# Sparse attention feeding an ELU feed-forward layer: a new plan for the opening and for the first chunk

## The chip, the cores and the metric

The kernel runs on one core of a Trainium2 chip. The metric is the device time of one execution in microseconds (us). The core has a matrix engine (TensorE, PE in the profile), a vector engine (VectorE, DVE), a scalar engine (ScalarE, ACT), a general engine (GpSimd, POOL), which here issues nearly all loads, and SyncE (SP), which issues the stores. Each engine runs its instructions in the order of the program; semaphores hold an instruction until what it needs is there.

## The reference

Eight batches of eight heads, 576 positions, head size 64. Heads 0 to 3 see the last 32 positions ("local"), heads 4 to 7 see every 32nd position before their own ("strided"). The result is the input of a feed-forward layer with an ELU between two products.

```python
scores = scale * np.matmul(q, k.transpose(0, 1, 3, 2))
mask_local = (rel >= 0) & (rel < stride)
mask_strided = (rel >= 0) & (pos[None, :] % stride == pos[:, None] % stride)
...
attn = np.exp(scores)
attn = attn / (np.sum(attn, axis=-1, keepdims=True) + 1e-09)
out = np.matmul(attn, v)
...
x = out.transpose(0, 2, 1, 3).reshape(B * S, H * D)     # 4608 x 512
h = x @ w_in                                            # 512 x 2048
g = np.where(h > 0.0, h, alpha * (np.exp(np.minimum(h, 0.0)) - 1.0))
return g @ w_out                                        # 2048 x 512
```

Inputs and output are float32; products are in bf16.

## The kernel before

**Attention.** Each batch has four pairs of heads: S0, S1 (strided) and l0, l1 (local); in the opening the first batch's are written s0, s1, l0, l1 and the second batch's strided ones S0, S1. A `Pair` has these steps. `t_q` and `t_k` transpose q and k on TensorE (lines 360 to 387) and copy the result out of PSUM, mostly by ScalarE. `s0` and `s1` (`scores`, line 488) are the products of the first and second part of the blocks, with an exp on ScalarE (line 508); `m0`, `m1` multiply by the mask on VectorE (line 523; from the second batch on the mask follows its score by itself). `a0`, `a1` (`av`, line 527) multiply by v, take a reciprocal and scale on VectorE (lines 550, 551). `x` (`x_out`, line 566) transposes the result into `xT`, the input of the feed-forward layer, with a copy on ScalarE, or on VectorE from the third batch on. `v_in` (line 416) copies the strided heads' v from `v_raw` into `v_str`, which has a column of ones behind each block; ScalarE does it for the second batch and VectorE from the third. `halo` (line 423) copies the last 32 rows of each local v block to where the next block finds them.

**Feed-forward layer.** The 4608 tokens are worked in nine chunks of 512. In step s of chunk nb, `moe_in` (line 640) makes four matmuls of 128x512 for 128 columns of the hidden layer, and `moe_act` (line 652) the ELU: an exp on ScalarE (line 655), then a TENSOR_SCALAR (line 662) and a TENSOR_TENSOR (line 664) on VectorE; for five steps of chunk 0 (`ON_SCALAR`) a Relu on ScalarE (line 658) and one instruction on VectorE (line 659) instead. `moe_out` (line 668) makes four matmuls of the second product. `outs` (line 746) says which of them stand behind a step: of chunk 0, number 0, 1 and 2 behind its steps 11, 13 and 15; from then on one behind each step, the other 13 of a chunk in the chunk after it.

**The order of the work** is written by hand. `OPENING` lists the steps of the first batch and the first transposes of the second; `fill` are matmuls without use, `moe.c` the products of feature block c for the first three steps of chunk 0 ("ahead", line 633). Then the loop of line 755 runs the chunks: while chunk nb is worked, batch nb + 1 is prepared, its steps put into gaps: gap 2s stands ahead of step s, gap 2s + 1 behind its ELU. `attention` (line 597) fills the gaps by `TIMES`: a first gap, a distance between pairs, and offsets of the steps. For the second batch the pairs start at the gaps 3, 9, 15, 21; for the third at 4, 10, 16, 22, with v_in at the start.

**PSUM.** The banks go round in rings: `sc` for scores, `hps` for `moe_in` (three banks in the first ten steps of chunk 0, then two), `ops` for `moe_out`, `ring` for the rest. A step that takes a bank waits for whoever read it last.

**Loads.** GpSimd issues them in this order, all in its one queue: the first batch's k, q, v (its strided q comes by SyncE), a quarter of w_in (`load_w_in(0)`), then lines 327 to 334 for the second batch, quarters 1 and 2 of w_in among them; after the opening quarter 3, the four quarters of w_out, and the third batch (line 739). `load_strided` issues five DMAs per tensor, `load_local` one. Quarter i of w_in serves the steps 4i to 4i + 3 of each chunk.

```python
    load_w_in(0)
    load_strided(1, "q")
    load_w_in(1)
    load_strided(1, "k")
    load_strided(1, "v")
    load_local(1, "q")
    load_local(1, "k")
    load_local(1, "v")
    load_w_in(2)
```

Of the kernel before, what the change touches and what calls it, by code (L numbers as in the profile page):

```python
# [32 lines left out]
PIECES = (-2, -1, 0, 2, 3, 5, 7, 0)  # L33
TIMES = (
    None,
    (3, 6, (-3, -2, 0, 2, 4, 6, 9, 3)),
    (4, 6, (-3, -2, 0, 2, 4, 6, 8, 0)),
    (2, 7, PIECES),
    ((2, 8, 15, 22), 0, PIECES),
)  # L40

OPENING = """
s0.cast_q s0.t_q s0.t_k s1.cast_q s1.t_k s0.s0 s0.m0 s1.t_q s0.s1 s0.m1 fill.2 l0.t_q s1.s1
s1.m1 s1.s0 s1.m0 l0.t_k l1.t_q fill.1 s0.v l0.s0 l0.m0 l1.t_k l0.s1 s1.a0 s0.a0 l0.m1 l1.s0
s1.a1 s0.a1 fill.1 l1.s1 l1.m0 fill.1 s1.halo s1.x fill.1 s0.x l1.m1 fill.1 l0.a0 fill.1 l0.a1
l1.a0 moe.2 l1.a1 S0.t_q l0.x S1.t_q moe.3 l1.x moe.0 moe.1
""".split()  # L50
ON_VECTOR = "s0.t_q s1.cast_q s1.t_k l0.t_q s0.v l1.x".split()

# [6 lines left out]
def kernel(  # L59
# [9 lines left out]
    nc = tc.nc  # L69
    B, H, S, D = q.shape  # L70
# [44 lines left out]
    def share(sc, hps, ops, ring):  # L115
        rings.update(sc=Ring(*sc), hps=Ring(*hps), ops=Ring(*ops), ring=Ring(*ring))
# [9 lines left out]
    def bf16_bank():  # L126
# [14 lines left out]
    v_str = [consts.tile([128, 4, 5, D + 1], BF16, tag=f"v_str{i}", name=f"v_str{i}")  # L141
             for i in range(3)]
# [23 lines left out]
    raw = {}  # L166
    src = {"q": q, "k": k, "v": v}

    def load_strided(b, name, engine=nc.gpsimd, heads=range(4)):
        rows = src[name][b, 4:8].rearrange("h (t r) d -> h t r d", r=STRIDE)  # L170
        if b == 0 and name in stage:
            t = stage[name]
        elif name == "v":
            if b not in raw:
                raw[b] = p_raw.tile([128, 4, 5, D], BF16, tag="v_raw", name="v_raw")
            t = raw[b]
        else:
            t = nat[name, "str"][b % 3].rearrange("p (h g d) -> p h g d", h=4, d=D)
        for h in heads:
            engine.dma_start(out=t[0:108, h].rearrange("p g d -> p (g d)"),  # L180
                             in_=rows[h, :, 0:30, :].rearrange(
                                 "t (r g) d -> t r (g d)", g=5))
            if h == 1:
                engine.dma_start(
                    out=t[108:126, :, 0:2, :].rearrange("p h g d -> p h (g d)"),
                    in_=rows[:, :, 30:32, :].rearrange("h t g d -> t h (g d)"))

    def load_local(b, name):
        if name == "v":

            nc.gpsimd.dma_start(
                out=v_loc[b % 3][32:128, :, :, :D].rearrange("p h i d -> p (h i) d"),
                in_=v[b, 0:4].rearrange("h (i p) d -> p (h i) d", p=LB))
            return
        flat = nat[name, "loc"][b % 3]
        if b < EARLY:
            nc.gpsimd.dma_start(
                out=flat[0:LB].rearrange("p (h x) -> p h x", h=4),
                in_=src[name][b, 0:4].rearrange("h (p j) d -> p h (j d)", j=L_RUN))
            return  # L200
        t = flat[:, 0:20 * D].rearrange("p (a i e d) -> p a i e d", a=2, i=5, d=D)
        for h in range(4):
            nc.gpsimd.dma_start(  # L203
                out=t[:, h // 2, 0:4, h % 2],
                in_=src[name][b, h, 0:512].rearrange("(i p) d -> p i d", p=128))
        for a in range(2):
            nc.gpsimd.dma_start(
                out=t[0:64, a, 4],
                in_=src[name][b, 2 * a:2 * a + 2, 512:576].rearrange("h p d -> p h d"))
# [20 lines left out]
    def load_batch(b):  # L230
        for name in "qkv":
            load_strided(b, name)
        for name in "qkv":
            load_local(b, name)

    def rows_of(t, h):

        return t[0:126, h, 0:2, :], t[0:108, h, 2:5, :]
# [83 lines left out]
    def load_w_in(i):  # L322
        nc.gpsimd.dma_start(out=w_in_sb[:, :, 512 * i:512 * (i + 1)],
                            in_=wi[:, :, 512 * i:512 * (i + 1)])

    load_w_in(0)
    load_strided(1, "q")
    load_w_in(1)
    load_strided(1, "k")
    load_strided(1, "v")  # L330
    load_local(1, "q")
    load_local(1, "k")
    load_local(1, "v")
    load_w_in(2)


    class Pair:
# [228 lines left out]
        def x_out(self):  # L566
# [22 lines left out]
            else:  # L589
# [4 lines left out]
                        identity[0:LB, 0:LB])  # L594
                self.copy("x", self.b > 1)(dst, xt[:, 0:S])

    def attention(b, start, pitch, at):


        gaps = {}  # L600
        pairs = [Pair(b, s, hp) for s in (b < LATE, b >= LATE) for hp in range(2)]
        begin = start if b >= LATE else [start + pitch * i for i in range(4)]
        if b >= LATE:
            gaps[begin[0]] = [pairs[3].halo]
        for i, pr in enumerate(pairs):
            if b == 1 and pr.strided:
                pr.t_q = lambda: None
            for off, piece in ((at[0], pr.t_q), (at[1], pr.t_k),
                               (at[7], lambda pr=pr: pr.v_in(0)),
                               (at[7] + (b > 1), lambda pr=pr: pr.v_in(1)),  # L610
                               (at[2], lambda pr=pr: pr.scores(0)),
                               (at[3] if b < WHOLE else at[2] + (b < LATE),
                                lambda pr=pr: pr.scores(1)),
                               (at[4], lambda pr=pr: pr.av(0)),
                               (at[5] - (b >= LATE and i == 0),
                                lambda pr=pr: pr.av(1)),
                               (at[6] + (b > 1 and pr.strided) + (b >= LATE), pr.x_out), (at[5] - 2, pr.halo if b < LATE else lambda: None)):
                gaps.setdefault(begin[i] + off, []).append(piece)
        return gaps
# [86 lines left out]
    def run(gaps, keys):  # L706
        for gap in sorted(g for g in gaps if g in keys):
            for piece in gaps[gap]:
                piece()

    every = range(-10, 1000)
    pairs = {p.name: p for p in (Pair(0, s, hp) for s in (True, False) for hp in range(2))}
    pairs.update((f"S{hp}", Pair(1, True, hp)) for hp in range(2))
    parts = [s for s in OPENING if s.startswith("moe")]
    for step in OPENING:
        pair, what = step.split(".")
# [29 lines left out]
    def outs(nb, s):  # L746

        if nb == 0:
            return [(0, i) for i in range(3) if s == 11 + 2 * i]
        step = [(nb - 1, i) for i in range(3, MC)]  # L750
        if nb < n_chunks:
            step += [(nb, i) for i in range(3)]
        return step[s:s + 1]

    for nb in range(n_chunks + 1):

        if nb + 1 < B:
            gaps = attention(nb + 1, *TIMES[min(nb + 1, 4)])
            if nb == 0:
                share([pair_a], b_halves + singles[3:], [], singles[:3])  # L760
            elif nb + 1 < LATE:
                share([pair_a], b_halves, singles[3:], singles[:3])
            else:
                share([pair_a], b_halves + singles[:1], singles[3:], singles[1:3])
        else:
            gaps = {}
            share([], b_halves + singles[:1], singles[2:], singles[1:2])
        if nb + 3 < B:
            load_batch(nb + 3)
        for s in range(MC):  # L770
            if nb == 0 and s == 10:
                share([pair_a], b_halves, singles[3:], singles[:3])
            if s == (9 if nb + 2 > LATE else 6) and nb > 0 and nb + 2 < B:
                transpose_batch(nb + 2, int(nb + 2 >= LATE))
            if s == 13 and nb + 2 == EARLY:
                transpose_batch(nb + 2, 2)
            run(gaps, (2 * s,) if s else range(-10, 1))
            late = LATE <= nb + 1 and s + 1 < MC
            if nb < n_chunks:
                moe_in(nb, s)  # L780
            if nb < n_chunks and not late:
                moe_act(nb, s)
            run(gaps, (2 * s + 1,) if s + 1 < MC else range(2 * s + 1, 1000))
            if nb < n_chunks and late:
                moe_act(nb, s)
            if nb == B and s == 4:
                range_flag(row_ok16)
            for chunk, i in outs(nb, s):
                moe_out(chunk, i)
        if nb + 1 == B:  # L790
            row_ok16 = range_check()
# [163 lines left out]
```

## Time and profile before

| what | us |
|---|---|
| median of 3 runs (325.82 to 325.88) | 325.88 |
| the profiled execution | 325.9 |
| its span, first to last instruction | 324.0 |
| TensorE busy (2198 matmuls) | 302.3 |
| VectorE busy | 244.7 |
| ScalarE busy | 175.3 |
| GpSimd busy, DMA issues among it | 139.0 |
| DMA: bytes moved | 36.33 MB |

Busy times are sums over the span. "Idle before" an instruction is the time in which its engine had nothing running, and the arrow behind it names what ended that time. In the table of stretches each engine has its busy us and its number of instructions; the granted clock of TensorE (1.00 is full) and what the DMA engines moved follow. The transfers of a GpSimd DMA run after its issue has ended. The opening lasts until about 27 us, chunk 0 to 54.78, chunk 1 to 91.49.

### The profile page before, as it was taken

Reading aid. Unit: us, or ns where it says so; the run is one execution under the profiler, and the core shown is the slowest. Engines: PE = TensorE matmul, PEld = TensorE weight load, DVE = VectorE, ACT = ScalarE, POOL = GpSimd, SP = SyncE. Lnnn points to the kernel's source line nnn. Section 1 sums busy time; section 2 is a strip of 40 time slices with the busy share of each in tenths; the row PEclk is TensorE's granted clock in tenths of the full one; section 3 lists DMA queues with packets and bytes.
Section 4 is the critical chain, followed back from the end, with each engine's and each line's share of the span. In section 5 each row is a group of like instructions: output and inputs, shape, how many; then the busy total and the mean of one; then the engine's idle time right before and its main releaser. Section 6 shows DMA issues by size and latency. Waiting matters only on the chain.

```text
span 324.0 us, 6040 instructions
## 1 busy us (share of the span) xinstructions
PE 302.3 (93%) x2198; PEld 148.2 (46%) x2198; DVE 244.7 (76%) x539; ACT 175.3 (54%) x333; POOL 139.0 (43%) x218
## 2 busy tenths in 40 slices
PE   0887799999999999999999999999999999999993
PEld 0553454455544544444444444444445444444441
DVE  6586986687988988989798879887987666766600
ACT  3668876776545544556645655555565444344310
POOL 9769725968938849968933930000000000000000
PEclk9979999999999999999999999999999999999998
DMA  6999999999999999999994993391110000100012
GB/s 103 156 179 130 172 207 124 149 136 160 119 118 184 148 144 183 75 153 172 215 129 88 141 211 66 81 149 51 53 51 34 33 32 34 65 33 33 34 67 72
DMA packets 108826, 36.33 MB, mean 112 GB/s; under 512 B 87341, under 2 KB 104181, under 8 KB 108789
## 3 DMA queue, kind: packets, MB, share of 16 engines
q0 software_dynamic: 71632, 18.10, 63.1%
q1 hardware_dynamic: 37157, 17.77, 27.2%
q8 instruction: 19, 0.31, 0.4%
q14 instruction: 18, 0.15, 0.2%
HBM read 36.70 MB, written 9.44 MB: 142 GB/s over the span
## 4 chain that ended last, share of the span: by engine, by line
PE 69%; DMA 11%; DVE 9%; POOL 6%; ACT 3%; issue 1%; ACTq 0%; POOLq 0%; DVEq 0%
PE single L674 32%; PE half L629 22%; PE single L629 8%; DMA w_out_sb<-in_moe_w_out_dram 6%; DVE g_sb L664 3%; DVE e_sb L662 2%; DMA q_str<-in_q_dram 2%; PE single L542 2%; DMA k_str<-in_k_dram 2%; DVE x_l L551 1%; PE pair_a L463 1%; POOL v_raw L180 1%; ACT e_sb L655 1%; DMA v_raw<-in_v_dram 1%; POOL k_str L180 1%
## 5 line engine op out<-in xcount | busy, mean ns | idle before, releaser
L674 PE MATMUL single<-w_out_sb,g_sb 128*128 128x512 bf16 x576 | 146.0, 379 | 0.4 <-DVE g_sb L664 0.4
L629 PE MATMUL half<-xT,w_in_sb 128*128 128x512 bf16 x436 | 112.5, 379 | 0.5 <-DVE g_sb L664 0.3
L655 ACT ACTIVATE e_sb<-half 128x512 f32<-128x512 f32 x109 | 65.4, 600 | 69.2 <-PE half L629 67.9
L662 DVE TENSOR_SCALAR e_sb<-e_sb 128x512 bf16<-128x512 f32 x139 | 64.0, 460 | 35.5 <-ACT e_sb L655 35.0
L674 PEld LDWEIGHTS <-g_sb 128*128 128x128 bf16 x576 | 53.5, 98 | 59.6 <-DVE g_sb L664 1.1
L629 PEld LDWEIGHTS <-w_in_sb 128*128 128x128 bf16 x576 | 52.0, 98 | 58.0 <-issue 1.8
L664 DVE TENSOR_TENSOR g_sb<-e_sb,half 128x512 bf16<-128x512 bf16 x104 | 71.5, 688 | 3.6
L629 PE MATMUL single<-xT,w_in_sb 128*128 128x512 bf16 x140 | 36.5, 379 | 1.3 <-DMA w_in_sb<-in_moe_w_in_dram 1.3
L655 ACT ACTIVATE e_sb<-single 128x512 f32<-128x512 f32 x35 | 21.0, 599 | 25.1 <-PE single L629 23.1
L678 ACT COPY o_sb<-single 128x512 f32<-128x512 f32 x36 | 21.1, 588 | 17.9 <-PE single L674 17.8
L542 PEld LDWEIGHTS <-pr 128*128 128x128 bf16 (+3 forms) x352 | 20.4, 103 | 15.5 <-DVE pr L523 1.0
L469 ACT ACTIVATE pr<-pair_a 126x936 bf16<-126x936 f32 (+1 forms) x20 | 19.2, 962 | 12.8 <-PE single L463 12.8
L664 DVE TENSOR_TENSOR g_sb<-e_sb,single 128x512 bf16<-128x512 bf16 x35 | 24.1, 688 | 1.2
L180 POOL DMA_DIRECT2D k_str<-in_k_dram x32 | 20.0, 644 | 9.6 <-issue 3.0
L180 POOL DMA_DIRECT2D v_raw<-in_v_dram x32 | 19.9, 648 | 9.1 <-DVE v_str L421 7.4
L180 POOL DMA_DIRECT2D q_str<-in_q_dram x28 | 17.9, 669 | 5.8 <-DMA w_out_sb<-in_moe_w_out_dram 2.0
L551 DVE TENSOR_TENSOR x_l<-single,rden 96x384 bf16<-96x384 f32 x32 | 17.7, 554 | 1.1
L551 DVE TENSOR_TENSOR x_s<-single,rden 126x256 bf16<-126x256 f32 (+1 forms) x32 | 15.7, 490 | 1.1
L203 POOL DMA_DIRECT2D q_loc<-in_q_dram x20 | 15.5, 817 | 1.9 <-DMA v_raw<-in_v_dram 0.9
L508 ACT ACTIVATE pr<-pair_a 128x576 bf16<-128x576 f32 (+2 forms) x20 | 13.1, 655 | 5.6 <-PE pair_a L500 5.6
L203 POOL DMA_DIRECT2D k_loc<-in_k_dram x20 | 15.3, 798 | 1.1 <-issue 0.8
L550 DVE RECIPROCAL rden<-single 96x6 f32<-96x6 f32 (+2 forms) x64 | 11.9, 185 | 3.1 <-PE single L542 2.4
(114 smaller groups left out, 257.0 us busy)
## 6 DMA issues: line engine op xcount, KB each, us to landing
out_dram<-o_sb SPq DMA_DIRECT2D x36, 256.0 KB, 3.2
v_loc<-in_v_dram POOLq DMA_DIRECT2D x8, 288.0 KB, 8.3
k_str<-in_k_dram POOLq DMA_DIRECT2D x32, 67.5 KB, 5.0
v_raw<-in_v_dram POOLq DMA_DIRECT2D x32, 67.5 KB, 4.5
w_in_sb<-in_moe_w_in_dram POOLq DMA_DIRECT2D x4, 512.0 KB, 9.4
w_out_sb<-in_moe_w_out_dram POOLq DMA_DIRECT2D x4, 512.0 KB, 17.1
q_str<-in_q_dram POOLq DMA_DIRECT2D x28, 67.5 KB, 7.2
q_loc<-in_q_dram POOLq DMA_DIRECT2D x20, 64.0 KB, 5.4
```

Of the source, the lines that this page charges most:

```text
L180: engine.dma_start(out=t[0:108, h].rearrange("p g d -> p (g d)"), in_=rows[h, :, 0:30, :].rearrange("t (r g) d -> t r (g d)", g=5))
L203: nc.gpsimd.dma_start(out=t[:, h // 2, 0:4, h % 2], in_=src[name][b, h, 0:512].rearrange("(i p) d -> p i d", p=128))
L469: nc.scalar.activation(both, sc[0:nk, :, 0:w], ACT.Exp, scale=scale)
L508: nc.scalar.activation(halves, sc[0:nk, :, 0:w], ACT.Exp, scale=scale)
L542: nc.tensor.matmul(av[0:m, p, blk - b0, :], lhsT=pr[0:nk, o:o + m], rhs=vt[0:nk, 2 * self.hp + p, blk, :], start=True, stop=True)
L551: nc.vector.tensor_tensor(self.x[0:nq, b0:b0 + n].rearrange("q g p d -> q p g d"), av[0:nq, :, 0:n, 0:D], r.unsqueeze(3).to_broadcast([nq, ...
L629: nc.tensor.matmul(hps, lhsT=w_in_sb[:, c, m * 128:(m + 1) * 128], rhs=xT[:, c, nb * N_TILE:(nb + 1) * N_TILE], start=start, stop=stop)
L655: nc.scalar.activation(e_sb, hps, ACT.Exp)
L662: nc.vector.tensor_scalar(e1_sb, e_sb, scalar1=1.0, scalar2=1.0, op0=ALU.min, op1=ALU.subtract)
L664: nc.vector.tensor_tensor(g_of[nb][:, m, :], e1_sb, hps, op=ALU.max)
L674: nc.tensor.matmul(ops, lhsT=g_of[nb][:, m, kk * 128:(kk + 1) * 128], rhs=w_out_sb[:, m, :], start=(m == 0), stop=(m == MC - 1))
L678: nc.scalar.copy(o_sb, ops)
```

## The change

Four things change together.

- The loads: the second batch's strided k and v are issued ahead of quarter 1 of w_in, and quarter 2 of w_in ahead of the local v. Between the local k and quarter 2 of w_in, GpSimd copies the second batch's v from `v_raw` to `v_str`, in two instructions; before, ScalarE did this in chunk 0.
- The opening: the halo of the first batch moves ahead of l1's second scores, l1.m1 behind l0.a1, one `fill` is dropped, S1.t_q moves to the end, and S0.t_k and S0.s0 of the second batch come in from chunk 0.
- The second batch's other steps in chunk 0 follow a list of their own, `SECOND`, of gaps and steps. `attention` is no longer called for it.
- The third batch's pairs start at the gaps 8, 13, 18, 23. `moe_out` number 0 and 1 of chunk 0 stand behind steps 13 and 15, number 2 moves into chunk 1, which has two of them behind step 12. `hps` keeps three banks for the first twelve steps of chunk 0.

```diff
 TIMES = (
     None,
-    (3, 6, (-3, -2, 0, 2, 4, 6, 9, 3)),
-    (4, 6, (-3, -2, 0, 2, 4, 6, 8, 0)),
+    None,
+    (8, 5, (-3, -2, 0, 2, 4, 6, 8, 0)),
...
+SECOND = """
+1 S1.t_k 3 S0.s1 7 S0.a0 7 S1.s0 9 S0.a1 10 S1.s1 11 S1.a0 12 S0.x 13 l0.t_q 14 S1.a1 15 l0.t_k
+17 S1.x 17 l0.s0 18 l1.t_q 19 l1.t_k 20 l0.s1 22 S1.halo 22 l1.s0 23 l0.a0 25 l0.a1 25 l1.s1
+26 l1.a0 28 l0.x 28 l1.a1 31 l1.x
+""".split()
...
-s1.a1 s0.a1 fill.1 l1.s1 l1.m0 fill.1 s1.halo s1.x fill.1 s0.x l1.m1 fill.1 l0.a0 fill.1 l0.a1
-l1.a0 moe.2 l1.a1 S0.t_q l0.x S1.t_q moe.3 l1.x moe.0 moe.1
+s1.a1 s0.a1 s1.halo fill.1 l1.s1 l1.m0 fill.1 s1.x fill.1 s0.x fill.1 l0.a0 l0.a1 l1.m1
+l1.a0 moe.2 l1.a1 l0.x S0.t_q moe.3 l1.x S0.t_k moe.0 moe.1 S0.s0 S1.t_q
...
     load_strided(1, "q")
-    load_w_in(1)
     load_strided(1, "k")
     load_strided(1, "v")
+    load_w_in(1)
     load_local(1, "q")
     load_local(1, "k")
+    for o, i in zip(rows_of(v_str[1][:, :, :, 0:D], slice(0, 4)),
+                    rows_of(raw[1], slice(0, 4))):
+        nc.gpsimd.tensor_copy(o, i)
+    load_w_in(2)
     load_local(1, "v")
-    load_w_in(2)
...
+    def second():
+        pairs.update((f"l{hp}", Pair(1, False, hp)) for hp in range(2))
+        gaps = {}
+        for gap, step in zip(SECOND[::2], SECOND[1::2]):
+            pair, what = step.split(".")
+            gaps.setdefault(int(gap), []).append(
+                lambda p=pairs[pair], what=what: p.step(what))
+        return gaps
...
         if nb == 0:
-            return [(0, i) for i in range(3) if s == 11 + 2 * i]
+            return [(0, i) for i in range(2) if s == 13 + 2 * i]
+        if nb == 1:
+            if s == 12:
+                return [(0, 14), (0, 15)]
+            return [(0, s + 2) if s < 12 else (1, s - 13)]
...
-            gaps = attention(nb + 1, *TIMES[min(nb + 1, 4)])
+            gaps = attention(nb + 1, *TIMES[min(nb + 1, 4)]) if nb else second()
...
-            if nb == 0 and s == 10:
+            if nb == 0 and s == 12:
                 share([pair_a], b_halves, singles[3:], singles[:3])
```

2 lines of the change are left out of this document (removed).

## The prediction, made before the changed kernel ran

> **What bounds the kernel now.** I read the page first (TensorE busy 93% of a span of 324.0 us, so everything is TensorE's idle time), then busy time by stretch, then who waited for whom in the stretch that the change rewrites. In the table the columns are TensorE, its weight loads, VectorE, ScalarE, GpSimd, each with busy us and instructions.
>
> ```profile
> PE   0887799999999999999999999999999999999993
> core 0: us, PE busy (x) PEld busy (x) DVE busy (x) ACT busy (x) POOL busy (x), PEclk, DMA share, GB/s
> 28.00:36.00 8.00, 5.53 (x64) 2.91 (x64) 7.71 (x17) 7.70 (x15) 7.88 (x13) 1.00 1.64 144
> 36.00:44.00 8.00, 6.74 (x96) 3.91 (x91) 6.67 (x15) 6.42 (x14) 3.93 (x5) 1.00 1.27 203
> 44.00:54.78 10.78, 9.72 (x78) 5.00 (x77) 8.88 (x20) 7.69 (x15) 3.04 (x6) 1.00 1.10 170
> 54.78:91.49 36.71, 36.26 (x307) 18.66 (x306) 28.29 (x61) 23.22 (x41) 30.93 (x50) 1.00 1.36 137
> ```
>
> 54.78 and 91.49 are the first matmuls of chunks 1 and 2. Chunk 1 leaves TensorE 0.45 us idle: from there on, work moved in costs its full length. Chunk 0 has 2.47 + 1.26 + 1.06 = 4.8 us idle, and that is all there is to win. From 28 to 36 VectorE (7.71 of 8) and ScalarE (7.70) are the bound, later it is mixed. TensorE's waits of 20 to 54.78, and what VectorE met:
>
> ```profile
> PE single L629 <- DMA w_in_sb<-in_moe_w_in_dram: 1.3, 1, 1.3
> PE single L591 <- DVE x_l L551: 1.0, 2, 0.8
> PE pair_a L500 <- ACT pr L508: 0.9, 2, 0.7
> PE pair_a L500 <- ACT kT_str L371: 0.8, 1, 0.8
> PE single L542 <- ACT v_str L421: 0.5, 1, 0.5
> ...
> 28.98 0.86 DVE L662 TENSOR_SCALAR e_sb<-e_sb 128x512 bf16<-128x512 f32 x1
> 61.71 0.81 DVE L421 COPY v_str<-v_raw 126x512 bf16<-126x512 bf16 x1 [1.80 <-DMA v_raw<-in_v_dram]
> ...
> 17.19 0.82 POOL L323 DMA_DIRECT2D w_in_sb<-in_moe_w_in_dram  x1
> 18.89 0.60 POOL L180 DMA_DIRECT2D k_str<-in_k_dram  x1 [0.87 <-DMA v_loc<-in_v_dram]
> 20.75 0.57 POOL L180 DMA_DIRECT2D k_str<-in_k_dram  x1 [1.26 <-DMA w_in_sb<-in_moe_w_in_dram]
> 28.40 1.19 POOL L191 DMA_DIRECT2D v_loc<-in_v_dram  x1
> 29.57 1.53 POOL L323 DMA_DIRECT2D w_in_sb<-in_moe_w_in_dram  x2
> 35.91 1.44 POOL L245 MEMSET q_str<- 32x1280 bf16 x1
> ```
>
> Each wait of GpSimd's queue is on the DMA issued eight before it, so only eight loads are in flight; strided ones also cost GpSimd 0.6 us each, and at 26 to 28 us, with only these, the DMA moved 94 GB/s instead of the 205 of the weights.
>
> **The change, part by part.** Chunk 0 is walked in three stretches, with durations of the rows of before.
>
> Loads. W_in(1) moves behind the five k and the five v loads. These still wait for the same landings (18.8 v_loc, 20.7 w_in(0), 21.9 q_str), so k gains only the slot at 17.2 and v lies 0.6 us earlier: last issue near 25.5, landing some 2.5 us later (the shortest v_raw landing), near 28.3. W_in(1), which landed at 24.9 and is needed by chunk 0's step 4 (31.67 before), goes out near 26.1 and needs its issue of 0.8, some 2 us until it flows, and 0.5 MB at 205 GB/s = 2.5 us: 30 to 31.4. Then q_loc, k_loc, the GpSimd copies, w_in(2), v_loc, w_in(3), and w_out as before. W_in(2) landed at 40.4, behind v_loc at 38.9; now before v_loc, near 37 to 38, and step 8 asks at 38.5: the wait of 1.26 goes. While GpSimd copies, w_in(1), q_loc and k_loc are still in flight (1.1 MB, over 5 us), so the DMA does not run dry, and w_out comes as before or up to 1.5 us earlier.
>
> The copies of v: two on ScalarE (0.63 + 0.83) become two on GpSimd, 512 and 768 elements per partition. The trace has no GpSimd copy. Lower bound: its memset of 1280 elements, 1.16. Upper: its affine select, 0.29 for 128 elements, by elements 2.9. I take 1.7, nearer the memset, which is the row with as many elements. They wait for the last v landing at 28.3, so end near 30.0; S0.a0 is wanted by TensorE near 30.3 (step 3 starts when VectorE has done e0, near 29.4, and takes 0.86). Behind them in GpSimd's queue stand w_in(2) and all later loads; cover: step 8 is at 38.5. If the copies end later, TensorE stands, but VectorE has a backlog until 33.0 and feels nothing up to about 31.
> The Trainium skill, "SBUF — State Buffer", Who interferes with whom, says that GpSimd and a VectorE copy or tensor_scalar in its fast two-port form exclude each other for a whole instruction. The rows fit it: one L662 took 0.86 beside 0.41 to 0.43 elsewhere, while GpSimd wrote a DMA's descriptors, and the q_str memset took 1.44 against 1.16 for k_str's. By it, the sum would be up to 1.3 us higher (two blocked operations of some 0.65).
>
> Opening, until chunk 0's first exp. S0.t_k (matmuls 0.44, ScalarE copy 0.68) and S0.s0 (0.28, exp 0.60, mask 0.41) come forward; cover on TensorE: moe.0 and moe.1 (0.65 each) lie between, which removes the waits of 0.8 (kT_str) and 0.7 (pr). The halo copy (ScalarE 1.26) starts at v_loc's landing, 18.85 instead of 19.81; l1.s1's exp slips from 19.14 to 20.1; s0.x's copies end at 21.9 instead of 22.2. L1.m1 stands behind l0.a1, so l1.a1's x is ready at 24.1 instead of 24.6. TensorE then does l1.x, S0.t_k, moe.0, moe.1 until 26.4 (27.45 before). But on ScalarE S0.s0's exp (26.7) and S1.t_q's copy (27.2) now stand ahead of chunk 0's first exp: 27.75 instead of 27.11, **0.6 later**. The dropped filler matmul (0.2) is not on this chain.
>
> 28 to 37.4. VectorE is bound. Before: 27.74 to 37.38 for e0 to e5 and the four S masks and two S0 results. Now from 28.3, without S0.m0 (0.33 from start to start): 28.3 + 9.64 - 0.33 = 37.6; without the stretched L662 37.2. **No gain**: TensorE's waits that are removed turn into waits for VectorE (its bank for step s comes free with g of step s-3).
>
> 37.4 to chunk 1. Before, 2.3 us idle (1.26 + 1.06). The w_in wait goes (-1.26). New: S1.halo (VectorE 0.49) now stands right ahead of l0.a0, and TensorE waits some 0.9; I leave the rest. TensorE's work shrinks by a moved output product (4 matmuls, 0.86) and by S1.a0, which is done earlier (0.2). Together -1.26 + 0.9 - 0.86 - 0.2 = **-1.4**: chunk 1 starts near 53.4.
>
> Chunk 1. The moved product comes back, where TensorE is full: **+0.86**. Batch 2's v copy moves from gap 4 to gap 8, 2 steps later (2 x 2.3 us), so VectorE's wait of 1.80 goes; of it TensorE felt only part of its 0.45 idle: **-0.3**. L1.x at gap 31 instead of 30 trades a wait of 0.3 (x_l) for one on VectorE's copy behind the step's g: 0. Pieces every 5 gaps squeeze batch 2 from 26 gaps into 23; VectorE, 28.29 of 36.71 busy there, stays below TensorE.
>
> Sum: the profiled execution took 325.9 (324.0 and 1.9 around it; median of the runs 325.88). 325.9 - 1.4 + 0.86 - 0.3 = **325.0**.
>
> **The rivals.**
> *More is won* (322.9). For: ScalarE loses 1.46 us of v copies in the stretch where it is busy 7.70 of 8; if chunk 0 is held by VectorE's work alone, it ends at 28.3 + 23.8 (24.17 busy from 27.7 to 55.9, less the mask) + 0.9 of small gaps = 53.0 instead of 55.9: -2.9 + 0.86 - 0.3 = -2.35, and with the first exp not later -0.6 more. Against: the list still puts ScalarE's copies in bunches (two t copies, S1.x's two and an exp between two steps).
> *The GpSimd copies hold up the opening* (327.3, the other side). Place: S0.a0, then all of TensorE, and VectorE's tensor_scalar. From 28.3 at the upper 2.9, and with operations of VectorE in its way (0.43 as at 28.98, once or twice) they end at 32 to 32.5; step 4 starts 1.0 to 1.5 late and VectorE, beyond its backlog, loses the same, plus 0.9 for its own blocked operations: 2.3 on the forecast. It decides from an end later than 31. Against: DMA issues and memsets beside VectorE stretched only three operations. That is the skill's rule above at its strongest.
> *Hidden anyway* (325.8). VectorE's stretch until 37.4 simply goes on, the wait for w_in(2) becomes one for VectorE's g, and the 0.86 comes back in chunk 1.
> *Not as it says*: the k loads gain one slot only, so S0.t_k at 24.8 might wait; its third load is issued at 20.75 and lands near 23.5. Within the range.
>
> **How the numbers follow.** Chances: forecast 0.40 (its own 324.2 to 325.7), more 0.22, hidden 0.12, slower 0.26. A measurement of this kernel tells 0.2% (0.65 us: 325.23 to 326.53) from no change. Faster: 0.30 of the forecast's and 0.22 = 0.52; same 0.10 + 0.12 = 0.22; slower 0.26. The range 323.0 to 327.2 takes in most of "more" and of "slower", and the bounds of the copies.
>
> **What would show it.** Right: no wait of L629 on w_in in steps 4 and 8; GpSimd's copies at 28 to 30.5; no wait on kT_str or pr before 35; VectorE without gaps from 28.3 to 37; chunk 1's first matmul near 53.4; no wait of v_str near 60. Wrong: a wait of S0.a0 on GpSimd over 0.8 us, L662 rows near 0.9 beside the copies, a wait at step 4 on w_in(1), chunk 1 not earlier than 54.3 (then slower or same) or before 52.5 (then more).

## The result and the profile after

The changed kernel takes 327.98 us (median of 11 runs, 326.12 to 329.28); the kernel before, on the same chip, 325.88 (324.27 to 327.15). The ratio is 1.0071, with a 95% interval of 1.0049 to 1.0093: 2.3 us slower, 1.6 to 3.0. The forecast was 325.0.

The profiled execution took 327.7, with a span of 325.8 instead of 324.0. The first view is the page's row of TensorE's busy tenths in 40 slices of the span, and the row of its granted clock.

```profile
PE   0885889999999999999999999999999999999993
...
PEclk9999699999999999999999999999999999999997
```

One slice is 8.1 us. The fifth, 32.6 to 40.7, has a clock of 0.6 only, right where the change was to win: from 32.2 on the clock is halved for 6.8 us. The next view is busy time by stretch; 56.86 and 94.13 are the first matmuls of chunks 1 and 2.

```profile
core 0: us, PE busy (x) PEld busy (x) DVE busy (x) ACT busy (x) POOL busy (x), PEclk, DMA share, GB/s
26.00:34.00 8.00, 3.81 (x38) 2.06 (x36) 6.07 (x11) 5.02 (x10) 7.48 (x10) 0.89 1.12 168
34.00:44.00 10.00, 9.65 (x95) 5.09 (x94) 6.83 (x17) 6.44 (x13) 5.95 (x10) 0.75 1.69 179
44.00:56.86 12.86, 11.13 (x105) 5.66 (x104) 11.30 (x25) 9.57 (x20) 4.79 (x9) 1.00 1.05 159
56.86:94.13 37.27, 36.76 (x311) 18.13 (x310) 29.42 (x61) 22.92 (x42) 30.92 (x50) 1.00 1.28 137
```

Chunk 1 starts at 56.86, where the forecast had 53.4 and the kernel before 54.78. It then takes 37.27 instead of 36.71, the 0.86 - 0.3 more that was forecast (but see the table: the agreement is luck of these two profiles). TensorE is busy 36.76 of it, so it is still full. In 26 to 34 TensorE idles for half of the time, and in 34 to 44 it is "busy" 9.65 of 10 at a clock of 0.75, which is work drawn out, not more work. Who waited for whom (TensorE, 26 to 58 us; total, times, longest):

```profile
PE half L645 <- DVE g_sb L680: 2.3, 1, 2.3
PE half L645 <- DMA w_in_sb<-in_moe_w_in_dram: 1.9, 1, 1.9
PE single L552 <- DVE v_loc L438: 0.9, 1, 0.9
```

L645 is `moe_in`'s matmul, L552 `av`'s. The first row stands ahead of step 3, the second ahead of step 4; the third is the halo's, foreseen at 0.9. TensorE's timeline of steps 3 to 5 (start, us, engine, line; in brackets the idle time before and what ended it):

```profile
30.18 1.02 PE L645 MATMUL half<-xT,w_in_sb 128*128 128x512 bf16 x4 [2.26 <-DVE g_sb L680]
...
33.47 1.89 PE L645 MATMUL half<-xT,w_in_sb 128*128 128x512 bf16 x4 [1.90 <-DMA w_in_sb<-in_moe_w_in_dram]
...
36.04 1.89 PE L645 MATMUL single<-xT,w_in_sb 128*128 128x512 bf16 x4
```

Four matmuls that take 1.02 at full clock took 1.89 twice behind the two idle stretches. The load that step 4 waits for, in the chain of waits (start, us):

```profile
24.70 8.72 DMA w_in_sb<-in_moe_w_in_dram
```

and GpSimd's timeline from its issue on:

```profile
24.70 0.96 POOL L330 DMA_DIRECT2D w_in_sb<-in_moe_w_in_dram  x1
25.49 0.86 POOL L204 DMA_DIRECT2D q_loc<-in_q_dram  x1
26.18 0.84 POOL L204 DMA_DIRECT2D k_loc<-in_k_dram  x1
27.55 1.58 POOL L342 COPY v_str<-v_raw 126x512 bf16<-126x512 bf16 x2 [0.52 <-DMA v_raw<-in_v_dram]
```

W_in(1) was issued at 24.70, sooner than forecast, and landed 8.72 us later, at 33.4, not at 30 to 31.4; two more loads followed it at once. GpSimd's copies of v were as forecast: 1.58 us, done at 29.1.

One execution can't be laid beside another to a microsecond here: the same kernel, profiled again (e11), starts chunk 1 1.6 us later. So the table gives several; the letters stand for runs that the next section explains. The columns are the start of the exp of chunk 0's steps 0, 3, 5, 8 and of chunk 1's first, chunk 0's length between the two first exps, chunk 1's, and the span, all in us and read from the traces.

| kernel | 0 | 3 | 5 | 8 | chunk 1 | length 0 | length 1 | span |
|---|---|---|---|---|---|---|---|---|
| before | 27.1 | 31.8 | 34.3 | 41.4 | 55.8 | 28.7 | 36.7 | 324.0 |
| before again (e11) | 27.8 | 32.5 | 36.3 | 42.9 | 57.5 | 29.7 | 36.3 | 324.2 |
| e7, before, no wait at step 8 | 27.3 | 32.0 | 35.8 | 41.3 | 57.0 | 29.7 | 35.9 | 323.6 |
| g4, before, clears moved | 28.3 | 33.0 | 35.5 | 41.5 | 57.1 | 28.8 | 35.9 | 323.4 |
| e6, before, outputs replanned | 27.5 | 32.2 | 34.7 | 41.6 | 55.9 | 28.4 | 37.3 | 324.3 |
| **after** | 28.0 | 31.2 | 38.0 | 43.2 | 57.9 | 29.9 | 37.3 | 325.8 |
| e9, after, no wait at step 4 | 29.1 | 32.3 | 36.5 | 43.1 | 57.8 | 28.7 | 37.8 | 326.2 |
| f1, after, clears on VectorE | 29.1 | 33.2 | 37.2 | 43.0 | 57.8 | 28.7 | 37.3 | 325.9 |
| g1, after, all three away | 29.4 | 32.5 | 35.4 | 43.3 | 58.1 | 28.6 | 37.3 | 326.0 |
| g2, after, own data | 29.0 | 32.1 | 35.0 | 42.9 | 57.8 | 28.8 | 37.4 | 325.7 |

Of the profiles that the table leaves out, chunk 0 takes 28.6 (f2), 28.8 (e4) and 29.6 (e8) with the old list, and chunk 1 35.9 to 36.4. With the new list chunk 0 takes 28.1 (e1), 29.5 to 30.3 (e2, e3, e10), and 30.9 to 31.8 (e5, g3, e12), and chunk 1 37.3 to 38.7 (e12, with the old outputs, 36.7).

The half clock is part of this scatter. E11 and the first profile of before are one kernel, and their first four exps are equally spaced; then e11 has half clock for 3.4 us (from 31.9 on) and before has none in chunk 0, and e11's chunk is 0.9 longer. E7 has such a piece too, g4, e6, e4 and f2 have none there. Each of e9, f1, g1 and g2 has one, the changed kernel two in a row.

From chunk 2 on all kernels run nearly alike (32.7 to 33.2 for chunk 2, then 31.5 to 32.1 each, the last but one 27.6); the trace of before that the prediction read spent 1.2 us more in its chunks 2 to 5 than e11.

### The profile page after: what moved, and what is told of

It is laid out like the page before. It is cut to its first block, busy times and chain, and to the rows that moved or that the text cites. A ratio compares the mean times of both kernels' runs of the same rounds, so it can differ in the third digit from the quotient of the medians.

```text
span 325.8 us, 6035 instructions
## 1 busy us (share of the span) xinstructions
PE 302.8 (93%) x2197; PEld 147.6 (45%) x2197; DVE 244.8 (75%) x539; ACT 172.9 (53%) x331; POOL 140.7 (43%) x220
## 4 chain that ended last, share of the span: by engine, by line
PE 78%; DMA 7%; DVE 6%; ACT 3%; POOL 3%; issue 1%; ACTq 0%; POOLq 0%
PE single L690 36%; PE half L645 26%; PE single L645 9%; DMA w_in_sb<-in_moe_w_in_dram 5%; PE single L552 3%; DVE g_sb L680 2%; DMA k_str<-in_k_dram 2%; PE pair_a L473 2%; ACT e_sb L671 1%; DVE e_sb L678 1%; DVE x_l L561 1%; PE single L588 1%; POOL k_str L187 1%; POOL v_raw L187 1%; PE pair_a L510 1%
## 5 line engine op out<-in xcount | busy, mean ns | idle before, releaser
L645 PE MATMUL half<-xT,w_in_sb 128*128 128x512 bf16 x432 | 112.4, 382 | 4.2 <-DVE g_sb L680 2.3
L678 DVE TENSOR_SCALAR e_sb<-e_sb 128x512 bf16<-128x512 f32 x139 | 63.8, 459 | 35.6 <-ACT e_sb L671 35.0
L645 PEld LDWEIGHTS <-w_in_sb 128*128 128x128 bf16 x576 | 52.7, 99 | 61.0 <-issue 4.4
L645 PE MATMUL single<-xT,w_in_sb 128*128 128x512 bf16 x144 | 38.4, 386 | 0.0
L671 ACT ACTIVATE e_sb<-single 128x512 f32<-128x512 f32 x36 | 21.7, 603 | 24.9 <-PE single L645 22.8
L552 PEld LDWEIGHTS <-pr 128*128 128x128 bf16 (+3 forms) x352 | 20.3, 103 | 15.7 <-issue 2.0
L680 DVE TENSOR_TENSOR g_sb<-e_sb,single 128x512 bf16<-128x512 bf16 x36 | 24.8, 688 | 1.2
```

What stands on the lines that cost most here:

```text
L552: nc.tensor.matmul(av[0:m, p, blk - b0, :], lhsT=pr[0:nk, o:o + m], rhs=vt[0:nk, 2 * self.hp + p, blk, :], start=True, stop=True)
L645: nc.tensor.matmul(hps, lhsT=w_in_sb[:, c, m * 128:(m + 1) * 128], rhs=xT[:, c, nb * N_TILE:(nb + 1) * N_TILE], start=start, stop=stop)
L671: nc.scalar.activation(e_sb, hps, ACT.Exp)
L678: nc.vector.tensor_scalar(e1_sb, e_sb, scalar1=1.0, scalar2=1.0, op0=ALU.min, op1=ALU.subtract)
L680: nc.vector.tensor_tensor(g_of[nb][:, m, :], e1_sb, hps, op=ALU.max)
```

## The experiments

Where a number is a ratio, it is to the kernel before on the same chip, with its 95% interval. The first question was which of the new waits costs the 2 us.

**e1, the load order of w_in(1) undone.**

```diff
 load_strided(1, "q")
+load_w_in(1)
 load_strided(1, "k")
 load_strided(1, "v")
-load_w_in(1)
```

> The changed kernel with one line put back: quarter 1 of w_in is loaded ahead of k and v again, all else as changed. Theory 'late weights' (step 4 waits 1.9 us for w_in(1), and the idle time brings the TensorE clock to 0.50 for 5 to 6 us): no wait of L645 on w_in at step 4, the clock at 1.00 from 28 to 40, chunk 1 starts at 53.5 to 54.5 instead of 56.86, time 324.3 to 325.5. Rival 'GpSimd copy' and rival 'late first exp' (TensorE idle 28.0 to 30.2 because ScalarE does S0.s0's exp and S1.t_q's copy first): unchanged within 0.5 us of 327.9, since neither is touched.

Measured: 327.92, 1.0077 [1.0042, 1.0112]. The wait at step 4 is gone, but in its place stands this one, in the opening (TensorE's timeline of e1; the first row in it is `S0.t_k`):

```profile
26.92 0.43 PE L378 MATMUL single<-identity,k_str 126*128 126x126 bf16 x5 [1.53 <-DMA k_str<-in_k_dram]
```

The first exp moved to 30.0. Ahead of step 4, the DMA has both k and w_in(1) to bring, and in these two profiles whichever is second is waited for: `S0.t_k` in the opening made k urgent.

**e2, v copied by ScalarE again** (at gap 6 of `SECOND`, the two GpSimd copies dropped).

```diff
-1 S1.t_k 3 S0.s1 7 S0.a0 ...
+1 S1.t_k 3 S0.s1 6 S0.v 7 S0.a0 ...
...
-    nc.gpsimd.tensor_copy(o, i)
```

> The changed kernel, but v of the second batch copied by ScalarE in gap 6 as before, not by GpSimd. 'Late weights': w_in(1) is issued ahead of the copies and lands near 33.4 as it did; time 327.5 to 328.7. Rival 'GpSimd copy': the time falls below 326.5, TENSOR_SCALAR rows near 29 to 31 are all below 0.5 us.

Measured: 328.48, 1.0108 [1.0059, 1.0157]. Nothing comes back: GpSimd's copies aren't the cause of the loss.

**e3, filler matmuls ahead of steps 3 and 4,** nine and eight, to keep TensorE's clock up.

```diff
+if nb == 0 and m == 3:
+    for _ in range(9):
+        nc.tensor.matmul(rings["ring"].peek(), lhsT=identity, rhs=mask_l[:, 0:512], ...)
+if nb == 0 and m == 4:
+    for _ in range(8):
+        nc.tensor.matmul(hps, lhsT=identity, rhs=mask_l[:, 0:512], ...)
```

> The changed kernel with 17 filler matmuls without use: 9 ahead of step 3 into a free bank and 8 ahead of step 4 into that step's own bank, where TensorE stands idle at 28.0 to 30.2 and 31.6 to 33.5; all waits stay. Theory 'clock' (the half clock from 32.6 to 38.9 is the larger part of the loss): clock 1.00 from 28 to 40, chunk 1 starts about 2 us earlier (54.5 to 55.3), time 325.7 to 326.5. Rival 'waits alone' (VectorE or the late data set the pace, the slow clock is hidden): time 327.3 to 328.5.

Measured: 329.22, 1.0147 [1.0087, 1.0206]. The clock was 1.00 throughout chunk 0, and step 4 to step 5 took 1.4 us instead of 2.6. Yet TensorE then waited elsewhere, for VectorE's x of the strided heads (its waits, 26 to 58 us):

```profile
PE single L558 <- DVE x_s L567: 1.4, 1, 1.4
PE single L594 <- DVE x_s L567: 0.9, 1, 0.9
```

**e4, e6, e7, e8: one part of the change alone, in the kernel before.** E4 has w_in(1) behind k and v; e6 the outputs, the banks and the third batch's gaps; e7 w_in(2) ahead of the local v; e8 v by GpSimd.

```diff
-load_w_in(1)                    # e4: three lines lower
+load_w_in(1)
-(4, 6, (-3, -2, 0, 2, 4, 6, 8, 0)),    # e6
+(8, 5, (-3, -2, 0, 2, 4, 6, 8, 0)),
-return [(0, i) for i in range(3) if s == 11 + 2 * i]
+return [(0, i) for i in range(2) if s == 13 + 2 * i]
...
-load_local(1, "v")              # e7: behind load_w_in(2)
+load_local(1, "v")
+    nc.gpsimd.tensor_copy(o, i)    # e8
```

> The kernel before with one line moved: quarter 1 of w_in behind the second batch's strided k and v, nothing else of the change. 'Late weights': w_in(1) lands at 33 to 34, step 4, at 31.67 before, waits 1.5 to 2 us; time 327.0 to 328.5, the slow clock perhaps with it. Rival (the order of the loads is free, the loss is in the rest of the plan): 325.6 to 326.3.

> The kernel before with the change's outputs (two of chunk 0's products in chunk 0, the third in chunk 1 as a second one behind step 12), three banks for 12 steps and the third batch from gap 8 every 5 gaps; nothing else. Forecast's terms: chunk 0 not shorter by the whole 0.86, chunk 1 longer by 0.86 less 0.3: chunk 1 starts 0 to 0.9 earlier and lasts 37.1 to 37.6; time 325.3 to 326.4. Rival 'late list': the third batch's later and denser steps cost chunk 1 more, 38 or over; time 327 or over.

> The kernel before with quarter 2 of w_in ahead of the local v of the second batch, nothing else. Theory: the wait of 1.3 us at step 8 (L629 on w_in) goes or falls below 0.4, and VectorE's and ScalarE's own work hides half of it: time 324.6 to 325.3 where before measures 325.3 to 325.9. Rival 'hidden': within 0.3 us of before.

> The kernel before with v of the second batch copied by GpSimd between the local k and the local v, nothing else. Theory 'GpSimd copy harmless': copies of about 1.6 us in all, TENSOR_SCALAR rows beside them up to 0.9; ScalarE loses 1.46 us of work in gap 6: time 324.9 to 325.9. Rival 'GpSimd copy' (port and queue): w_in(2) lands later and step 8 waits 2 us or more, time 326.5 to 327.5.

Measured: e4 325.82, 1.0029 [1.0000, 1.0059]; e6 326.55, 1.0054 [1.0017, 1.0091]; e7 326.4, 1.0043 [1.0011, 1.0074]; e8 326.85, 1.0047 [1.0014, 1.0080]. No part wins anything. Three of them lose 0.43 to 0.54% each alone, where the whole change loses 0.71%; so their prices don't add up. These three are set against the same runs of the kernel before, and that kernel against itself (e11) came out at 1.0016, so a price of 0.4% is near the limit of the comparison. In e4 step 4 waits only 0.2 us for w_in(1), not the 1.5 to 2 that were expected.

E7 matters most. The wait for w_in(2) at step 8, the 1.26 that the forecast took off, is gone. Its profile is best laid beside e11's: both have a piece of half clock at the same place, and up to step 7 their exps lie equally far behind the first, to 0.1 us (step 7 12.59 in both). Here is TensorE at step 8 in e11, and between the steps 8 and 9 in e7:

```profile
41.82 1.04 PE L629 MATMUL single<-xT,w_in_sb 128*128 128x512 bf16 x4 [1.01 <-DMA w_in_sb<-in_moe_w_in_dram]
```

```profile
41.52 0.30 PE L500 MATMUL pair_a<-qT_loc,kT_loc 64*128 64x96 bf16 x6 [0.30 <-ACT pr L508]
...
42.73 0.32 PE L578 MATMUL single<-identity,x_s 108*128 108x108 bf16 x3 [0.69 <-DVE x_s L551]
```

Without the wait of 1.01 step 8's exp comes 14.1 instead of 15.1 us behind the first, 1.0 sooner. Then TensorE waits 0.30 for ScalarE's exp and 0.69 for VectorE's x_s, which e11 doesn't have there, and step 9's exp is at 17.2 in both. What w_in held up, VectorE and ScalarE hold up one step later.

E6 shows chunk 1's part by itself (busy time by stretch, the columns as above):

```profile
54.81:92.10 37.29, 36.37 (x306) 18.17 (x311) 28.81 (x61) 22.76 (x41) 30.79 (x50) 1.00 1.30 133
```

37.29, as in the changed kernel, though the opening and the list of chunk 0 are those of before.

**e5, the opening's early scores undone too** (e1, and S0.t_k, S0.s0, S1.t_q back where they had been, the S pairs' other steps too).

```diff
-l1.a0 moe.2 l1.a1 l0.x S0.t_q moe.3 l1.x S0.t_k moe.0 moe.1 S0.s0 S1.t_q
+l1.a0 moe.2 l1.a1 S0.t_q l0.x S1.t_q moe.3 l1.x moe.0 moe.1
```

> The changed kernel with two parts put back: w_in(1) ahead of k and v, and S0.t_k, S0.s0, S1.t_q where they were (S0.t_k and S0.s0 in gaps 1 and 3, the S pairs' other steps in the gaps of before); GpSimd's copy of v, w_in(2) ahead of v_loc, the late local steps, the outputs and batch 2 as changed. Theory 'early scores': k is wanted in the opening and w_in(1) at step 4, eight DMAs in flight cannot bring both, so either order costs 1.5 to 1.9 us, and S0.s0's exp ahead of chunk 0's first exp delays step 3: then step 5 starts at 33 to 34 (36.0 in the changed one), chunk 1 at 54 to 55, time 325 to 326. Rival 'late list' (the later steps, the moved product and batch 2 cost it): step 5 earlier but chunk 1 still at 56 or later, time 327 to 328.5.

Measured: 328.79, 1.011 [1.0059, 1.0161]. The first exp is at 27.1, and step 5 at 33.9 is the earliest of all. Then step 6 comes only at 38.5: TensorE had waited twice, 1.85 us in all, for VectorE's x_s, and from 35.6 on it ran at half clock for 6.8 us. What had been won is lost again within one step.

**e9 and e10, no wait for w_in(1) by other data.** Steps 4 to 7 of chunk 0 use quarter 0 of w_in, so that part of the result is another. E10 also has S0.s0 and S1.t_q behind the first exp, and S1.t_k one gap later.

```diff
 def moe_chunk(nb, m, c, hps, start, stop):
+    if nb == 0 and 4 <= m < 8:
+        m -= 4
```

> The changed kernel, but steps 4 to 7 of chunk 0 multiply by quarter 0 of w_in instead of quarter 1 (other data, so that part of the result is another), so that nothing of chunk 0 waits for w_in(1); the same loads and the same work. Theory 'late weights' (the wait of 1.9 us at step 4 and the half clock behind it): step 4's exp at 33 to 33.5 (35.4 in the changed one), the half clock gone or half as long, chunk 1's first exp at 55 to 56 (57.9), time 325.5 to 326.5. Rival 'chain' (VectorE's and ScalarE's list sets the pace anyway, the wait was cover for it): chunk 1's first exp at 57 or later, time 327.2 or over.

> As the run with quarter 0 in steps 4 to 7 (that part of the result is another), and besides S0.s0 and S1.t_q behind chunk 0's first exp (gap 1), S1.t_k in gap 3. Theory 'late first exp': the first exp at 26.9 to 27.2 instead of 28.0, step 3 at 29.4 to 29.8, TensorE's wait of 2.3 for VectorE's g at step 3 below 1.5, time 0.5 to 0.9 below that run. Rival 'chain': equal within 0.3 us.

Measured: e9 327.3, 1.0055 [1.0026, 1.0084]; e10 327.06, 1.0061 [1.0031, 1.0090]. In e9 TensorE's first two waits are

```profile
PE half L647 <- DVE g_sb L682: 2.2, 1, 2.2
PE single L552 <- DVE x_s L561: 1.5, 1, 1.5
```

and step 8 is at 43.1, as in the changed kernel. In e10 chunk 0's first exp comes at 25.3, and TensorE then waits 2.1 for GpSimd's v_str, whose copies take 2.04 here. Chunk 1 still begins at 55.6, the earliest of all profiles, and then takes 38.3. The time is not below e9's, as its rival had it: the late first exp, taken away, gave nothing that can be measured.

**e11, the kernel before again,** to see what the comparison makes of no change.

> The kernel before, once more, for a second trace. If the 1.2 us that chunks 2 to 5 took more in the first trace (33.2, 31.8, 31.9, 31.6 against 32.7, 31.5 to 31.7, 31.45, 31.45 in all others) belong to that one execution: 32.7 and 31.45 here, time 325.0 to 325.9. If they belong to the kernel: the same excess.

Measured: 325.63, 1.0016 [0.9989, 1.0043].

**e12, the changed kernel with outputs, banks and third batch as before** (e6's diff, the other way).

> The changed kernel with the outputs, the three banks and the third batch's gaps as before; the opening, loads and second batch as changed. Forecast's term: chunk 1 lasts 36.7 instead of 37.3, chunk 0 0.3 to 0.9 longer; time within 0.5 us of 327.9. Rival (the later and denser third batch is a main cost): time 326.8 or less.

Measured: 328.34, 1.0078 [1.0039, 1.0116]. Chunk 1 takes 36.7 again, but in this profile step 4 waits 3.0 for w_in(1) and chunk 0 takes 31.8. The 0.6 that chunk 1 gives back can't be seen in the time.

The next theory, A below, was VectorE held off by GpSimd. In e1's VectorE timeline one operation of 0.43 us takes seven times as long, while GpSimd issues v_loc's load and clears six pads of q_loc, k_loc (`clear_loc`) back to back; in the kernel before, VectorE stood still for v_raw just then:

```profile
60.46 2.95 DVE L678 TENSOR_SCALAR e_sb<-e_sb 128x512 bf16<-128x512 f32 x1 [0.50 <-ACT e_sb L671]
```

TensorE feels it: among its waits of 57 to 97 us in e1 is this one, and e1's chunk 1 takes 38.7.

```profile
PE half L645 <- DVE g_sb L680: 1.2, 1, 1.2
```

The Trainium skill, "SBUF — State Buffer", Who interferes with whom, has a VectorE `tensor_scalar` in its two-port form and GpSimd exclude each other for a whole instruction; the row agrees in being stretched beside GpSimd, though it doesn't name the form. But 2.95 is several GpSimd instructions long, not one.

**f1 and f2: the clears that GpSimd did at 35 to 38 and near 62 us go to VectorE,** in the opening behind S0.t_k (f1, the changed kernel) or around l1.x (f2, the kernel before).

```diff
+        if pair == "clear":
+            if what == "1":
+                clear_v(2)
+                clear_nat(2)
+            else:
+                for i in range(3):
+                    clear_loc(i, nc.vector)
+            continue
-    clear_v(2, nc.gpsimd)
-    clear_nat(2, nc.gpsimd)
-    for i in range(3):
-        clear_loc(i, nc.gpsimd)
```

> The changed kernel with the 'clear' memsets (the last v and natural buffers, the three pairs of q_loc, k_loc) done by VectorE in the opening, instead of by GpSimd behind the v copies and, for the last ones, at 61.7 to 63.3 us. Theory A, VectorE held off by GpSimd's memsets is a good part of the loss: no TENSOR_SCALAR over 1 us between 58 and 66 us, chunk 1 from 37.3 to 36 or less, the span 1 to 1.5 us below the changed kernel's 327.98, near 326.7. Theory B, the loss is the pace of the new lists: the memsets' place is worth at most 0.3 us, 327.5 to 328.5.

> The kernel before with the same memsets on VectorE in the opening. Theory A: there VectorE waits for v_raw while they run at 60.7 to 62.4 us, so that little is lost to them; 0 to 0.7 us below before, chunk 1 at 36 to 36.7. Theory B: within 0.3 us of before. By both, a loss of more than 0.5 us would mean that the opening's VectorE has no room for the memsets.

Measured: f1 327.45, 1.0064 [1.0034, 1.0094]; f2 325.7, 1.0000 [0.9976, 1.0025]. The longest such operation near there is this in the changed kernel, and the second in f1:

```profile
62.00 1.62 DVE L678 TENSOR_SCALAR e_sb<-e_sb 128x512 bf16<-128x512 f32 x1 [0.46 <-ACT e_sb L671]
```

```profile
61.88 1.18 DVE L678 TENSOR_SCALAR e_sb<-e_sb 128x512 bf16<-128x512 f32 x1 [0.57 <-ACT e_sb L671]
```

Chunk 1 takes 37.28 from exp to exp in both. TensorE is the bound there, and VectorE has slack for 1.6 us. It has none for much more: where the operation takes 2.3 to 3.0 us (e1, e2, e3, e9, e10), chunk 1 takes 37.7 to 38.7, and TensorE waits 0.4 to 1.2 for g_sb. So theory A doesn't explain the changed kernel's profile in chunk 1, but it does explain the longer chunk 1 of these five. F2 shows no cost of the clears in the kernel before.

**g1 to g4: do the costs stand in for one another?** G1 takes three suspects from the changed kernel at once: e9's edit, nine fillers ahead of step 3, and the clears on VectorE where it idles at 9 to 25 us. G2 has the kernel's own data and e1's order instead of e9's edit. G3 is e5 with these clears, g4 the kernel before with them.

```diff
-s0.cast_q s0.t_q s0.t_k s1.cast_q s1.t_k s0.s0 s0.m0 s1.t_q
+s0.cast_q s0.t_q s0.t_k clear.k s1.cast_q s1.t_k clear.v s0.s0 s0.m0 clear.q s1.t_q
...
-s0.v l0.s0
+s0.v clear.l01 l0.s0
...
-l1.x
+clear.l2 l1.x
```

> The changed kernel with three suspects away at once: steps 4 to 7 of chunk 0 read quarter 0 of w_in (no wait for its load; part of the result is another), nine filler matmuls ahead of step 3 (no half clock), the clears on VectorE in idle places of the opening at 9 to 25 us (no memsets of GpSimd beside the ELU). Theory A, the loss of chunk 0 goes from one of these to the next when only one is taken away: step 3 to step 5 in 3 us (4.0 to 6.8 before), step 8 at 41 us or sooner, chunk 1 from 56 us, span 324, 326.2 median. Theory B, the new lists' own pace: step 8 at 43 us whatever is taken away, span 325.5 or more, 327.3 or more.

> The changed kernel with its own data, w_in's quarter 1 issued ahead of k and v again, nine fillers ahead of step 3, the clears as in g1. Theory A: the wait moves to the opening (k_str at 26.9), first exp at 29.5 to 30, from there steps as in g1: chunk 1 from 57 us, 327. Theory B: 327.5 to 328.5.

> e5 (w_in's quarter 1 early, S0's scores out of the opening and back in their gaps) with the clears on VectorE in the opening's idle places. e5 reached step 5 at 33.9 us, the earliest of all, and then lost 2 us at 34 to 36.5 behind a TENSOR_SCALAR that took 1.6 us over its 0.43, and the clock after it. Theory A: without GpSimd's memsets that wait and the half clock go; step 6 near 36.5 instead of 38.5, chunk 1 near 56, span 324.5, 326.3. Theory B: chunk 1 at 58 or later, 328 or more.

> The kernel before with the clears on VectorE in idle places of the opening, where f2 had them ahead of chunk 0's first exp (28.0 instead of 27.1 to 27.8 us). Theory A: first exp at 27.1 to 27.8, chunk 1 near 55.5, 0.3 to 1 us below before, faster than both kernels. Theory B, the memsets cost nothing where they were: within 0.3 us of before.

Measured: g1 327.14, 1.0058 [1.0033, 1.0083]; g2 327.23, 1.0060 [1.0031, 1.0088]; g3 327.55, 1.0056 [1.0026, 1.0086], with chunk 1 at 59.8 in its profile; g4 325.79, 1.0017 [0.9989, 1.0046].

G1's time lies just under theory B's 327.3, those of g2 and g3 between the two forecasts, and g4 is as theory B had it. In the profiles, step 3 to step 5 takes 2.9 us as theory A said (6.8 in the changed kernel's profile). Then step 5 to step 8 takes 7.9, against 5.2, and step 8 stands at 43 as theory B said. Here is g2 from its first ELU to step 6, by stretch (the columns as above), then by TensorE's waits (20 to 58 us), then in TensorE's timeline at step 6:

```profile
29.70:39.00 9.30, 7.43 (x51) 3.33 (x49) 9.03 (x20) 6.07 (x12) 8.22 (x11) 0.89 1.50 159
```

```profile
PE single L384 <- DMA k_str<-in_k_dram: 1.2, 1, 1.2
PE single L558 <- DVE pr L539: 0.9, 1, 0.9
...
PE single L594 <- DVE x_s L567: 0.9, 1, 0.9
```

```profile
37.35 1.91 PE L651 MATMUL half<-xT,w_in_sb 128*128 128x512 bf16 x4
```

VectorE is busy 9.03 of 9.30, and what TensorE waits for is VectorE's mask (L539) and x_s (L567). From step 0's g to step 5's VectorE needs 7.5 us in g1 and g2, against 8.1 in before, so the new list spares it 0.6 here. But in these two it starts on the ELU only when chunk 0's first exp is done, at 29.7 to 30.1, 2 us later than before (27.7). Up to step 6 VectorE is the wall.

The half clock is not out of the way, though. It comes behind the two waits, at 37.1 in g2 and 37.9 in g1, for 3.4 us, and g2's matmuls of step 6 take 1.91 instead of 1.04. So the stretch from step 5 to step 8 holds both, and the two runs don't separate them. Over all executions the clock can be told apart: its mean over a run is 0.988 in the changed kernel and 0.995 in g1 and 0.996 in g3, which is what the kernel before has (0.995), and g1 and g3 still lose 0.58 and 0.56%. Most of the loss needs no more half clock than before had. No version beats the kernel before; f2 and g4 can't be told from it.

## Why the prediction was wrong

**What was right.** The opening's first exp is later: 27.75 forecast, 28.0 measured. Over the changed kernel and four variants with the same opening (after, e2, e3, e9, e12) the mean is 28.2, over before, e6, e7, e8 and e11 27.3, so 0.9 instead of 0.6; e4, with the old opening and only the load order changed, has 28.1, so the opening isn't shown to be the whole of it. The halo's wait is 0.9. GpSimd's copies take 1.58 us against 1.7, a choice between wide bounds, and are done at 29.1. The wait for v_raw near 60 is gone.

**What failed first: "The w_in wait goes (-1.26)", in "37.4 to chunk 1".** The wait goes, and nothing comes of it: e7 has the step 1.0 us sooner and gives 0.30 + 0.69 back to ScalarE and VectorE before the next, and its ratio is over 1. The forecast took a wait that ended last at one matmul for time that could be had. Yet the paragraph before it had said of 28 to 37.4 that TensorE's removed waits turn into waits for VectorE; that holds behind step 8 too. With it goes the rest of the credit: between the first exps of chunks 0 and 1 the forecast needed 26.7 (55.84 - 1.4 - 27.75). The old list takes 28.4 to 28.8 in five of the six profiles without half clock there (before, e4, e6, f2, g4), and the new one 28.6 to 28.8 in e9, f1, g1 and g2, with an output product less; 28.1 (e1) is the shortest of all. E9, f1, g1 and g2 each have one piece of half clock, so whether the 0.86 was hidden, or was won and paid again to the clock, stays open. The rival "hidden anyway" named the failure, with 0.12, and left out the opening's cost.

**What failed second: "W_in(1) ... 30 to 31.4", in "Loads".** From issue to landing it took 8.72, not 0.8 + 2 + 2.5 = 5.3. Over the nine profiles with this order it took 6.1 to 8.7 and landed at 31.8 to 34.2. The 205 GB/s are those of 38 to 50 us (203 to 211 in every 2 us), when mostly weights were on the way; here v loads were issued ahead of the quarter and q_loc and k_loc behind it, and in 26 to 34 all loads together got 168. The profile of before had the number, in the page's list of DMA issues (median 9.4 us) and in the answer for w_in's tile:

```profile
w_in_sb<-in_moe_w_in_dram POOLq DMA_DIRECT2D x4, 512.0 KB, 9.4
```

```profile
DMA to landing us min/median/max: 7.7/9.4/12.5
```

The 7.7 is this very quarter, issued at 17.19 and landed at 24.9 by the prediction's own figures. From the forecast's issue at 26.1 it gives 33.8, and step 4 had been at 31.67 before. The Trainium skill, "DMA: Bandwidth & Descriptors", Anatomy of one DMA, gives a fit of 2.0 us + bytes / 436 GB/s; for 1 MB of float32 read that is some 4.4 us, an estimate by this fit, and the row of 9.4 differs.

**What failed third: "-0.3" in "Chunk 1".** The first pair of profiles gives 0.56 more, as summed, by luck. With the old plan chunk 1 takes 35.9 to 36.7, with a mean of 36.2 (before, e4, e7, e8, e11, f2, g4); with the new outputs 37.3 (after, e5, e6, f1, g1), 37.4 (g2), and more where the stretched operation comes in. So the plan costs some 1.1, the whole product and no credit.

**What went with the late load.** TensorE idled 2.26 us for VectorE's g, then 1.90 for w_in, within 6 us, and the half clock came, for 6.8 us from 32.2 on. The first of the two waits is no matter of the load: e9, which doesn't wait for w_in, has it too (2.2), with 3.4 us of half clock behind it. Chunk 0 takes 29.9 in the changed kernel's profile against 28.7, about 1.2. In the time the share is smaller: e9, f1, g1 and g2, with half of the half clock, have ratios of 1.0055 to 1.0064, against 1.0071, and the intervals overlap.

**The sum in the profiles' terms:** 0.9 for the opening, 0 to 1.2 for chunk 0, 1.1 for chunk 1; 2.0 to 3.2 against 2.3 (1.6 to 3.0) measured. This is bookkeeping of lengths: taking one of them away again (e10, e9, e12) didn't bring its time back. The forecast had the first and the last with 1.16 in all, and a credit of 2 in chunk 0 (26.7 against 28.7) that nothing pays. "More is won" fell with the same credit. The rival on the slower side (327.3) had the time almost right by luck and the cause wrong: GpSimd's copies end on time, and moving them back (e2) wins nothing.

**A row read too well.** The prediction set one L662 of 0.86 against 0.41 to 0.43 elsewhere. That trace has 14 of 139 over 0.5, this one among them, with two near by (0.54 at 30.8, 0.56 at 35.7) and the longest 1.17 at 85.2. The sum didn't hang on it.

**What stays open.** The parts don't add up: e6 alone has 1.0054, and the changed kernel without e6's part 1.0078. E4's, e7's and e8's prices alone (0.3 to 0.5%) aren't traced to one wait each; in e8's profile VectorE's TENSOR_SCALARs are stretched by 2.0 us in chunk 0, against 0.7 and 1.3 in the two of before. Whether e10's early chunk 1 would win, if the clears didn't stand beside its chunk 1, wasn't tried. G3's profile loses 1 us more than e5's, but its execution, 329.85, was one of the slowest of its twelve (median 327.55).

## What to carry to other kernels

When several engines are near their bound in a stretch, a wait that ends last at one place is not time to be won: sum the work of the next engine over the stretch first, from where it starts, and count only what lies beyond. For a load that is moved, take the time from issue to landing that the profile shows for that very load, under traffic, not its bytes over the best rate. Work pushed into a stretch where TensorE is full cost at least its whole length in the profiles here. And lay two profiles of one kernel side by side before a microsecond of one is explained: here they differ by 0.9 in chunk 0, which is about the half clock.

## What the hardware showed

- The half clock comes in pieces of 3.4 us: in chunk 0 there is one in e7, e9, e11, f1, g1 and g2, and there are two in a row (6.8) in the changed kernel, e2, e5 and e12. Ahead of it TensorE idled 2.26 and 1.90 us in the changed kernel, once 2.2 in e9 and 2.8 in f1, 0.92 and 0.86 in g1, and 0.78, 0.69 and 0.48 in e11; the profile of before has the last three idle stretches too (28.5 to 31.3) and no half clock behind them. The Trainium skill, "TensorE: Matmul & The Clock Gate", Part 1, has a window of 3413 ns and half rate; the trace agrees with both. Its rule in "Why this matters for your kernels", no idle gaps of over some 3 us, is too mild here: of all these only e12 has an idle stretch of 3.0.
- One piece of half clock cost some 0.9 us in chunk 0 of the kernel before (29.65 in e11, 28.73 without).
- A single VectorE `tensor_scalar` took 2.95 us against 0.43 when GpSimd issued a load and six memsets back to back. Where TensorE is the bound, 1.62 cost nothing (chunk 1 of the changed kernel 37.3, as with 1.18), and 2.95 held TensorE up for 1.2 us (e1).
- Filler matmuls kept the clock at 1.00 in chunk 0 (e3), and the kernel became slower, with a ratio of 1.0147 [1.0087, 1.0206]: TensorE waited 2.3 us for VectorE's x_s instead. A part of e3's loss is its chunk 1, 38.5 with an operation stretched to 2.74.
